# Windowed attention and a gated MLP block: a software pipeline over the batches, long-run loads of q and k, a transposed gating product and sink rows padded to 128

## The chip, the core and the metric

The kernel runs on one core of one Trainium2 chip. The metric is device time in microseconds (us), median of the runs; the kernel before takes 294.75 us (four runs, 294.15 to 295.45). Engines: PE is the tensor engine, PEld its weight loads, DVE the vector engine, ACT the scalar engine, POOL the GpSimd engine, SP the engine that here only issues transfers. In these kernels PE's results go to tiles in PSUM, and its operands lie in tiles in SBUF.

A run is called slow when it is over 1.5% above the fastest run of the same kernel. Times quoted as "measured" are medians of all runs, those marked slow included (the 401 and 452 us below left out); where that matters, the difference by fast runs stands beside it.

## The reference, cut to what matters

Four batches, eight heads, 768 positions, head width 64. Attention sees the last 128 positions and the first four (the sinks). The heads side by side are x (768 x 512 per batch), the input of a gated MLP.

```python
scores = scale * np.matmul(q, k.transpose(0, 1, 3, 2))
keep = is_sink | in_window            # first 4 positions, or 0 <= rel < 128
a = softmax(np.where(keep, scores, -1e9))
x = (a @ v), heads side by side
# gated block
h = gelu_tanh(x @ w_in)               # 512 -> 1024
u, v = h[..., :512], h[..., 512:]
v_n = (v - mean(v)) / np.sqrt(var(v) + 1e-06) * g_ln
v_s = np.einsum('ts,bsd->btd', w_sg, v_n) + b_sg[None, :, None]   # over positions
out = x + (u * v_s) @ w_out
```

(Softmax, gelu and the layer norm are abbreviated here.) q, k and v are drawn with a factor 0.1, so the scores are tiny and the softmax nearly flat.

## The kernel before

Everything is done in phases: attention of all batches, then the transposes of x and w_sg, then the first product of all batches, then the spatial and output products. The parts that the argument touches:

```python
# loads, per head pair: six casting transfers issued by POOL, 256-byte runs
nc.gpsimd.dma_start(
    out=q_sb[:, :, 64 * hl:64 * hl + 64],
    in_=q[b, h0 + hl, :, :].rearrange("(t p) d -> p t d", p=128),
)
# ... k, v likewise
qps = attn_ps.tile([128, S], BF16, name="qps", tag="trp")
for j in range(NT):
    nc.tensor.transpose(qps[:, 128 * j:128 * (j + 1)], q_sb[:, j, :], iden)
nc.vector.tensor_copy(qT, qps)                     # contiguous on both sides
# ... kT likewise, then scores, exp, mask multiply
# the four sink rows: a 4-row score product and 4-row AV products
nc.tensor.matmul(scs[0:n_sink, :], kT[ps, 0:n_sink],
                 qT[ps, 256:768], start=True, stop=True)
# ...
nc.tensor.matmul(av[:, i, :],
                 exs[:, 128 * (i - 2):128 * (i - 1)],
                 v_sb[0:n_sink, hl, 0, :],
                 start=False, stop=last)
```

In the gated block the kernel before applies gelu, `bn_stats` and `bn_aggr` per 128 rows, scales by 1/std in a later pass, forms `gated` with positions on the partitions, and so has to transpose it (96 transposes, 24 copies) before the output product.

The softmax here doesn't subtract the row's maximum and nothing guards it: scores larger than these inputs give would overflow.

Of the kernel before, what the change touches and what calls it, by code (L numbers as in the profile page):

```python
# [8 lines left out]
F32 = mybir.dt.float32  # L10
# [7 lines left out]
def kernel(  # L18
# [23 lines left out]
    assert S % 128 == 0  # L42
# [4 lines left out]
    assert window == 128  # L47
    scale = 1.0 / (Dh ** 0.5)

    consts = ctx.enter_context(tc.tile_pool(name="consts", bufs=1))  # L50
    x_pool = ctx.enter_context(tc.tile_pool(name="x_pool", bufs=1))
# [4 lines left out]
    def build_band_mask(dst, with_sink):  # L56
        nc.gpsimd.memset(dst[:, 0:128], 1.0)
        nc.gpsimd.affine_select(
            out=dst[:, 0:128], in_=dst[:, 0:128], compare_op=ALU.is_ge, fill=0.0,
            base=0, pattern=[[1, 128]], channel_multiplier=-1,  # L60
        )
        nc.gpsimd.memset(dst[:, 128:256], 1.0)
        nc.gpsimd.affine_select(
            out=dst[:, 128:256], in_=dst[:, 128:256], compare_op=ALU.is_ge, fill=0.0,
            base=-1, pattern=[[-1, 128]], channel_multiplier=1,
        )
        if with_sink:
            nc.gpsimd.memset(dst[0:n_sink, :], 1.0)

    m_grp0 = consts.tile([128, 512], BF16)  # L70
    build_band_mask(m_grp0[:, 0:256], True)
    build_band_mask(m_grp0[:, 256:512], False)
    m_grp = consts.tile([128, 512], BF16)
    build_band_mask(m_grp[:, 0:256], False)
    build_band_mask(m_grp[:, 256:512], False)

    x_sb = [x_pool.tile([128, NT, d_model], BF16, name=f"x_{b}") for b in range(B)]

    attn_sb = tc.alloc_tile_pool(name="attn_sb", bufs=2)
    attn_tmp = tc.alloc_tile_pool(name="attn_tmp", bufs=2)  # L80
    attn_ps = tc.alloc_tile_pool(name="attn_ps", bufs=2, space=bass.MemoryType.PSUM)
    attn_ps2 = tc.alloc_tile_pool(name="attn_ps2", bufs=3, space=bass.MemoryType.PSUM)

    for b in range(B):
        for hp in range(HP):
            h0 = 2 * hp
            q_sb = attn_sb.tile([128, NT, 128], BF16, name="q_sb")
            k_sb = attn_sb.tile([128, NT, 128], BF16, name="k_sb")
            v_sb = attn_sb.tile([128, 2, NT, 65], BF16, name="v_sb")
            nc.gpsimd.memset(v_sb[:, :, :, 64:65], 1.0)  # L90

            for hl in range(2):
                nc.gpsimd.dma_start(  # L93
                    out=q_sb[:, :, 64 * hl:64 * hl + 64],
                    in_=q[b, h0 + hl, :, :].rearrange("(t p) d -> p t d", p=128),
                )
                nc.gpsimd.dma_start(  # L97
                    out=k_sb[:, :, 64 * hl:64 * hl + 64],
                    in_=k[b, h0 + hl, :, :].rearrange("(t p) d -> p t d", p=128),
                )  # L100
                nc.gpsimd.dma_start(  # L101
                    out=v_sb[:, hl, :, 0:64],
                    in_=v[b, h0 + hl, :, :].rearrange("(t p) d -> p t d", p=128),
                )

            qT = attn_sb.tile([128, S], BF16, name="qT")
            kT = attn_sb.tile([128, S], BF16, name="kT")
            qps = attn_ps.tile([128, S], BF16, name="qps", tag="trp")
            for j in range(NT):
                nc.tensor.transpose(qps[:, 128 * j:128 * (j + 1)], q_sb[:, j, :], iden)  # L110
            nc.vector.tensor_copy(qT, qps)  # L111
            kps = attn_ps.tile([128, S], BF16, name="kps", tag="trp")
            for j in range(NT):
                nc.tensor.transpose(kps[:, 128 * j:128 * (j + 1)], k_sb[:, j, :], iden)  # L114
            nc.vector.tensor_copy(kT, kps)  # L115

            for hl in range(2):
                ps = slice(64 * hl, 64 * hl + 64)
                h = h0 + hl
                exa = attn_tmp.tile([128, NT, 256], BF16, name="exa", tag="exa")  # L120
                exps = [exa[:, j, :] for j in range(NT)]
                for g in range(NT // 2):
                    j0 = 2 * g
                    sc = attn_ps2.tile([128, 512], F32, name="sc_ps", tag="sc")
                    w = 0
                    for j in (j0, j0 + 1):
                        ncols = 256 if j < NT - 1 else 128
                        nc.tensor.matmul(sc[:, w:w + ncols],  # L128
                                         kT[ps, 128 * j:128 * (j + 1)],
                                         qT[ps, 128 * j:128 * j + ncols],  # L130
                                         start=True, stop=True)
                        w += ncols
                    nc.scalar.activation(out=exa[:, j0:j0 + 2, :].rearrange(  # L133
                        "p a b -> p (a b)")[:, 0:w], in_=sc[:, 0:w],
                        func=AF.Exp, scale=scale)
                    msk = m_grp0 if g == 0 else m_grp
                    nc.vector.tensor_mul(  # L137
                        exa[:, j0:j0 + 2, :].rearrange("p a b -> p (a b)")[:, 0:w],
                        exa[:, j0:j0 + 2, :].rearrange("p a b -> p (a b)")[:, 0:w],
                        msk[:, 0:w])  # L140
                scs = attn_ps2.tile([128, 512], F32, name="scs_ps", tag="sc")
                nc.tensor.matmul(scs[0:n_sink, :], kT[ps, 0:n_sink],  # L142
                                 qT[ps, 256:768], start=True, stop=True)
                exs = attn_tmp.tile([n_sink, 512], BF16, name="exs")
                nc.scalar.activation(out=exs, in_=scs[0:n_sink, :],  # L145
                                     func=AF.Exp, scale=scale)

                av = attn_ps2.tile([128, NT, 65], F32, name="av", tag="av")
                first = True
                for i in range(NT):  # L150
                    nc.tensor.matmul(av[:, i, :], exps[i][:, 0:128],  # L151
                                     v_sb[:, hl, i, :],
                                     start=first, stop=False)
                    first = False
                    if i >= 1:
                        nc.tensor.matmul(av[:, i, :], exps[i - 1][:, 128:256],  # L156
                                         v_sb[:, hl, i - 1, :],
                                         start=False, stop=False)
                    last = (i == NT - 1)
                    if i >= 2:  # L160
                        nc.tensor.matmul(av[:, i, :],  # L161
                                         exs[:, 128 * (i - 2):128 * (i - 1)],
                                         v_sb[0:n_sink, hl, 0, :],
                                         start=False, stop=last)
                    elif last:
                        pass
                rcp = attn_tmp.tile([128, NT, 1], F32, name="rcp")
                nc.scalar.copy(rcp, av[:, :, 64:65])  # L168
                nc.vector.reciprocal(rcp, rcp)  # L169
                nc.vector.tensor_mul(  # L170
                    x_sb[b][:, :, 64 * h:64 * h + 64],
                    av[:, :, 0:64], rcp.to_broadcast([128, NT, 64]),
                )

    attn_tmp.release()
    attn_sb.release()
    attn_ps2.release()
    attn_ps.release()

    w_in_sb = consts.tile([128, KD, d_ff], BF16)  # L180
    nc.gpsimd.dma_start(out=w_in_sb, in_=moe_w_in.rearrange("(c p) f -> p c f", p=128))
    w_out_sb = consts.tile([128, KU, d_model], BF16)
    nc.gpsimd.dma_start(out=w_out_sb, in_=moe_w_out.rearrange("(c p) f -> p c f", p=128))
    g_ln_sb = consts.tile([128, d_half], BF16)
    nc.gpsimd.dma_start(out=g_ln_sb, in_=moe_g_ln.partition_broadcast(128))
    b_sg_sb = consts.tile([128, NT], F32)
    nc.gpsimd.dma_start(out=b_sg_sb, in_=moe_b_sg.rearrange("(t p) -> p t", p=128))
    eps_sb = consts.tile([128, 1], F32)
    nc.vector.memset(eps_sb, 1e-6)

    gconst = ctx.enter_context(tc.tile_pool(name="gconst", bufs=1))
    wsgT = gconst.tile([128, NT, S], BF16)
# [4 lines left out]
    for ti in range(NT):  # L197
# [3 lines left out]
        for si in range(NT):  # L201
            nc.tensor.transpose(wps[:, 128 * si:128 * (si + 1)],
                                wsg_row[:, 128 * si:128 * (si + 1)], iden)
# [119 lines left out]
```

## Time and profile before

| stretch of the trace | what runs | us |
|---|---|---|
| 0 to 13 | start, first loads | 13 |
| 13 to 163 | attention of 16 head pairs, 9.4 us each | 150 |
| 163 to 184 | transposes of w_sg and x | 21 |
| 184 to 228 | first product, gelu, statistics | 44 |
| 228 to 294 | spatial and output products, stores | 66 |

First the page: the busy times, the row with PE's busy tenths, the row with the granted clock, and the chain of waits that ended last (by engine, then by line).

```profile
PE 263.8 (90%) x1545; PEld 129.8 (44%) x1556; DVE 165.1 (56%) x416; ACT 122.6 (42%) x236; POOL 91.1 (31%) x145
PE   0389999999999999999999387999996899999994
PEclk9999999999999999999999999999999799999999
PE 60%; DVE 16%; issue 12%; POOL 6%; DMA 3%; ACT 1%; ACTq 0%; POOLq 0%; DVEq 0%
```

PE is busy nine tenths of the span and has 60% of the chain, so PE bounds this kernel. But a busy PE can still be a slow one. The clock row reads full from the first slice on. The durations contradict it. These two lines are from the view of one tile's instructions (min/median/max in ns, then first and last start); both are 128x128 transposes of x.

```profile
L209 PE MATMUL wps<-iden,x_86 x24: 263/311/311, 174.2 to 177.4; 128*128 128x128 bf16 x24
L209 PE MATMUL wps<-iden,x_87 x24: 216/218/278, 177.5 to 180.2; 128*128 128x128 bf16 x24
```

The same instruction takes 311 ns up to 177.4 us and 218 ns from 177.5 us on. The trace's first clock record, one that reads full, is at 177.7 us; ahead of it there is none, and the row then assumes full speed. The transposes of q and k have a median of 311 ns too, in all of attention from 10.8 to 147.1 us. So the whole attention phase runs at half clock.

The second thing to see is what the four-row sink matmuls cost. The timeline (start in us, duration in us) around one row block of the AV product:

```profile
56.68 0.23 PE L161 MATMUL av<-v_sb,exs 4*128 4x65 bf16 x1
56.84 0.24 PE L151 MATMUL av<-v_sb,exa 128*128 128x65 bf16 x1
56.89 0.24 PE L156 MATMUL av<-v_sb,exa 128*128 128x65 bf16 x1
57.07 0.23 PE L161 MATMUL av<-v_sb,exs 4*128 4x65 bf16 x1
```

The durations overlap, so go by the starts. The two 128-row matmuls start 0.05 us apart; into and out of the four-row one it takes 0.16 to 0.18 us each. A row block takes 0.39 us; three starts 0.05 us apart would be 0.15 us, an estimate.

Last, one line of the groups, for the copy that brings transposed q from PSUM to SBUF (busy us, mean ns of one):

```profile
L111 DVE COPY qT<-qps 128x768 bf16<-128x768 bf16 x16 | 8.8, 550 | 20.2 <-PE qps L110 20.2
```

It takes 0.55 us.

### The profile page before, as it was taken

The numbers are of one execution on the slowest core, as the hardware profiler recorded it, in microseconds if no ns is written. First come the engines' busy times: TensorE is split into PE (matmuls) and PEld (weight loads), VectorE is DVE, ScalarE is ACT, GpSimd is POOL, SyncE is SP. The second block draws the span as 40 slices with busy tenths as digits, with TensorE's granted clock in tenths as the row PEclk, the third lists the DMA queues.
The fourth block names the chain that finished last, engine by engine and source line by source line (L and its number), as shares of the span: only waits on it lengthen the run. The fifth ranks groups of instructions, "written<-read, shape, count | busy, mean of one in ns | idle before, by whom it ended". The sixth has DMA issues, their size and how long they took to land.

```text
span 293.9 us, 4223 instructions
## 1 busy us (share of the span) xinstructions
PE 263.8 (90%) x1545; PEld 129.8 (44%) x1556; DVE 165.1 (56%) x416; ACT 122.6 (42%) x236; POOL 91.1 (31%) x145
## 2 busy tenths in 40 slices
PE   0389999999999999999999387999996899999994
PEld 0234454454445445444544265444442344445551
DVE  0145444364364445544644368499999933358884
ACT  1045545455454554645555000666567255530000
POOL 9993269385559556560301100000000000000000
PEclk9999999999999999999999999999999799999999
DMA  2999699999989899993443300000000000005574
GB/s 14 115 120 161 44 81 111 102 85 73 74 65 98 52 85 67 104 61 21 28 30 54 50 6 0 0 2 1 0 0 2 0 0 0 2 0 214 198 268 180
DMA packets 80836, 18.89 MB, mean 64 GB/s; under 512 B 75824, under 2 KB 77232, under 8 KB 80816
## 3 DMA queue, kind: packets, MB, share of 16 engines
q0 software_dynamic: 77360, 12.33, 57.1%
q1 hardware_dynamic: 3456, 6.29, 5.7%
q8 instruction: 12, 0.20, 0.3%
q14 instruction: 8, 0.07, 0.1%
HBM read 24.64 MB, written 6.29 MB: 105 GB/s over the span
## 4 chain that ended last, share of the span: by engine, by line
PE 60%; DVE 16%; issue 12%; POOL 6%; DMA 3%; ACT 1%; ACTq 0%; POOLq 0%; DVEq 0%
PE sc_ps L128 12%; PE vs_ps L264 11%; PE out_ps L282 7%; PE av L151 6%; DVE stats L242 5%; PE av L161 5%; PE scs_ps L142 4%; PE kps L114 4%; PE qps L110 3%; POOL v_sb L101 2%; PE av L156 2%; PE wps L209 2%; DVE mv L244 2%; POOL k_sb L97 1%; DVE vn_2082 L247 1%
## 5 line engine op out<-in xcount | busy, mean ns | idle before, releaser
L133 ACT ACTIVATE exa<-sc_ps 128x512 bf16<-128x512 f32 (+1 forms) x96 | 52.6, 562 | 44.4 <-PE sc_ps L128 43.7
L128 PE MATMUL sc_ps<-qT,kT 64*128 64x256 bf16 x192 | 54.4, 386 | 0.7 <-DVE kT L115 0.7
L151 PE MATMUL av<-v_sb,exa 128*128 128x65 bf16 x192 | 39.5, 242 | 0.0
L156 PE MATMUL av<-v_sb,exa 128*128 128x65 bf16 x160 | 38.1, 243 | 0.0
L137 DVE TENSOR_TENSOR exa<-exa,m_grp 128x512 bf16<-128x512 bf16 x64 | 24.1, 382 | 17.8 <-ACT exa L133 17.5
L93 POOL DMA_DIRECT2D q_sb<-in_q_dram x32 | 27.4, 858 | 16.1 <-PE qps L110 15.1
L97 POOL DMA_DIRECT2D k_sb<-in_k_dram x32 | 27.3, 859 | 10.4 <-PE qps L110 6.6
L161 PE MATMUL av<-v_sb,exs 4*128 4x65 bf16 x128 | 29.6, 231 | 0.6 <-ACT exs L145 0.6
L151 PEld LDWEIGHTS <-exa 128*128 128x128 bf16 x192 | 19.9, 115 | 18.6 <-issue 7.2
L110 PE MATMUL qps<-iden,q_sb 128*128 128x128 bf16 x96 | 17.4, 305 | 11.5 <-DMA q_sb<-in_q_dram 11.5
L101 POOL DMA_DIRECT2D v_sb<-in_v_dram x32 | 26.6, 840 | 1.3 <-POOL v_sb L90 1.3
L169 DVE RECIPROCAL rcp<-rcp 128x6 f32<-128x6 f32 x32 | 6.1, 192 | 32.4 <-ACT rcp L168 32.4
L264 PEld LDWEIGHTS <-wsgT 128*128 128x128 bf16 x144 | 14.4, 101 | 21.9 <-DVE vn_2082 L254 3.8
L282 PE MATMUL out_ps<-w_out_sb,gatedT 128*128 128x512 bf16 x92 | 22.0, 380 | 1.3 <-DVE gatedT L279 0.9
L137 DVE TENSOR_TENSOR exa<-exa,m_grp_66 128x512 bf16<-128x512 bf16 x32 | 13.6, 424 | 14.7 <-ACT exa L133 13.8
L145 ACT ACTIVATE exs<-scs_ps 4x512 bf16<-4x512 f32 x32 | 18.7, 585 | 5.6 <-PE scs_ps L142 5.2
L128 PEld LDWEIGHTS <-kT 64*128 64x128 bf16 x192 | 15.3, 112 | 12.8 <-issue 3.0
L111 DVE COPY qT<-qps 128x768 bf16<-128x768 bf16 x16 | 8.8, 550 | 20.2 <-PE qps L110 20.2
L168 ACT COPY rcp<-av 128x6 f32<-128x6 f32 x32 | 5.3, 164 | 34.7 <-PE av L161 34.7
L156 PEld LDWEIGHTS <-exa 128*128 128x128 bf16 x160 | 19.7, 124 | 0.0
L114 PE MATMUL kps<-iden,k_sb 128*128 128x128 bf16 x96 | 18.6, 304 | 0.8 <-DMA k_sb<-in_k_dram 0.8
L161 PEld LDWEIGHTS <-exs 4*128 4x128 bf16 x128 | 12.7, 99 | 14.2 <-issue 2.5
(188 smaller groups left out, 399.3 us busy)
## 6 DMA issues: line engine op xcount, KB each, us to landing
out_dram<-out_sb SPq DMA_DIRECT2D x24, 256.0 KB, 2.0
q_sb<-in_q_dram POOLq DMA_DIRECT2D x32, 96.0 KB, 3.4
k_sb<-in_k_dram POOLq DMA_DIRECT2D x32, 96.0 KB, 3.6
v_sb<-in_v_dram POOLq DMA_DIRECT2D x32, 96.0 KB, 3.6
wsg_row<-in_moe_w_sg_dram POOLq DMA_DIRECT2D x6, 192.0 KB, 3.6
w_in_sb<-in_moe_w_in_dram POOLq DMA_DIRECT2D x1, 1024.0 KB, 10.2
w_out_sb<-in_moe_w_out_dram POOLq DMA_DIRECT2D x1, 512.0 KB, 6.2
g_ln_sb<-in_moe_g_ln_dram POOLq DMA_DIRECT2D x1, 128.0 KB, 4.1
```

Source lines behind the costliest of these rows:

```text
L93: nc.gpsimd.dma_start(out=q_sb[:, :, 64 * hl:64 * hl + 64], in_=q[b, h0 + hl, :, :].rearrange("(t p) d -> p t d", p=128),)
L97: nc.gpsimd.dma_start(out=k_sb[:, :, 64 * hl:64 * hl + 64], in_=k[b, h0 + hl, :, :].rearrange("(t p) d -> p t d", p=128),)
L101: nc.gpsimd.dma_start(out=v_sb[:, hl, :, 0:64], in_=v[b, h0 + hl, :, :].rearrange("(t p) d -> p t d", p=128),)
L114: nc.tensor.transpose(kps[:, 128 * j:128 * (j + 1)], k_sb[:, j, :], iden)
L128: nc.tensor.matmul(sc[:, w:w + ncols], kT[ps, 128 * j:128 * (j + 1)], qT[ps, 128 * j:128 * j + ncols], start=True, stop=True)
L133: nc.scalar.activation(out=exa[:, j0:j0 + 2, :].rearrange("p a b -> p (a b)")[:, 0:w], in_=sc[:, 0:w], func=AF.Exp, scale=scale)
L137: nc.vector.tensor_mul(exa[:, j0:j0 + 2, :].rearrange("p a b -> p (a b)")[:, 0:w], exa[:, j0:j0 + 2, :].rearrange("p a b -> p (a b)")[:, 0:w],
L151: nc.tensor.matmul(av[:, i, :], exps[i][:, 0:128], v_sb[:, hl, i, :], start=first, stop=False)
L156: nc.tensor.matmul(av[:, i, :], exps[i - 1][:, 128:256], v_sb[:, hl, i - 1, :], start=False, stop=False)
L161: nc.tensor.matmul(av[:, i, :], exs[:, 128 * (i - 2):128 * (i - 1)], v_sb[0:n_sink, hl, 0, :], start=False, stop=last)
L264: nc.tensor.matmul(vs_ps, wsgT[:, si, 128 * t:128 * (t + 1)], vn_all[b][:, si, :], start=(si == 0), stop=(si == NT - 1))
L282: nc.tensor.matmul(out_ps, gatedT[:, 128 * c:128 * (c + 1)], w_out_sb[:, c, :], start=(c == 0), stop=(c == KU - 1))
```

## The change

The intent, in five parts:

1. **Pipeline over batches.** After batch 0's attention, each batch's spatial and output products are interleaved, unit by unit, with the next batch's attention. The first products (MV for the normed half, MU for the gate half) are interleaved with the transposes of the next batch's q and k (T).
2. **Long-run loads.** q and k are loaded so that partition p holds positions 6p to 6p+5, in runs of 1536 bytes, in f32, by SP; POOL casts them to bf16. The transposed result is then in the wrong order, and the copy out of PSUM puts it right by writing every sixth element.
3. **Transposed gating.** u and the spatial product are computed with features on the partitions, so the gated product needs no transposes. The multiplication by u is done on POOL.
4. **Padded sinks.** The four sink rows of all heads live in zero-padded 128-row tiles, so every AV operand has 128 rows; the row sums come from a head-selecting ones column.
5. 1/std is taken with a power on POOL, per two row blocks, at once.

Below, "first gated stage" is MV and MU of batch 0 with T of batch 1 and the transposes of w_sg; M1, M2, M3 are MV and MU of batches 1 to 3; "mixed" is a spatial and output stage with the next attention.

```diff
 # (cut to the core; the order of pieces is that of the new kernel)
-                nc.gpsimd.dma_start(
-                    out=q_sb[:, :, 64 * hl:64 * hl + 64],
-                    in_=q[b, h0 + hl, :, :].rearrange("(t p) d -> p t d", p=128),
-                )
+        q32 = stage.tile([128, 2, NT * Dh], F32, name="q32")
+        nc.sync.dma_start(out=q32, in_=q[b, hs].rearrange("h (p t) d -> p h (t d)", p=128))
 # ... k32 the same; v32 in short runs
-            nc.vector.tensor_copy(qT, qps)
+            pcast(cb.rearrange("p t h d -> p h t d"),
+                  src.rearrange("p h (t d) -> p h t d", d=Dh))
+            ps = ps_mm.tile([128, NT, 128], BF16, name="trp", tag="mm")
+            for t in range(NT):
+                nc.tensor.transpose(ps[:, t, :], cb[:, t, :, :].rearrange("p h d -> p (h d)"), iden)
+            dst = trs.tile([128, S], BF16, name=name + "T")
+            dv = dst.rearrange("p (i t) -> p t i", t=NT)
+            if name == "q":
+                nc.vector.tensor_copy(dv, ps)
+            else:
+                nc.scalar.copy(dv, ps)
 # ... padded sinks
-                                         exs[:, 128 * (i - 2):128 * (i - 1)],
-                                         v_sb[0:n_sink, hl, 0, :],
+                                 exs[b, p][:, 128 * (i - 2):128 * (i - 1)],
+                                 vsk[:, 2 * p:2 * p + 2, :].rearrange("p h d -> p (h d)"),
 # ... transposed gating
-            nc.scalar.activation(out=gated, in_=vs_ps, func=AF.Identity,
-                                 bias=b_sg_sb[:, t:t + 1])
-            nc.vector.tensor_mul(gated, gated, u_all[b][:, t, :])
-                nc.tensor.transpose(gps[:, 128 * c:128 * (c + 1)],
-                                    gated[:, 128 * c:128 * (c + 1)], iden)
+        nc.vector.scalar_tensor_tensor(out=tmp, in0=ps[:, 0:NH], scalar=g_sb[:, dc:dc + 1],
+                                       in1=b_bc[:, NH * hf:NH * (hf + 1)],
+                                       op0=ALU.mult, op1=ALU.add)
+        nc.gpsimd.tensor_mul(gatedT[b, hf][:, dc, :], tmp, uT[b][:, dc, NH * hf:NH * (hf + 1)])
 # ... the interleave
+        for n, a in enumerate(au):
+            a()
+            while done < ns and done * na < (n + 1) * ns:
+                su[done]()
+                done += 1
```

T, the transposes of w_sg and of x, the sink scores, the spatial and the output products share two PSUM slots (`ps_mm`, two buffers).

## The prediction

> **What bounds the kernel now.** The tensor engine (PE). The chain of waits gives it 60%. By stretches of the trace: attention 13 to 163 us with PE busy over 97%, that is 9.4 us per head pair; weight and x transposes 163 to 184, loosely filled; first product 184 to 228, where the vector engine's statistics chain has the chain of waits (38.7 of 41 us busy); spatial and output products 228 to 294. The load and the statistics are exposed because the phases are serial.
>
> Two things make the attention slow on PE.
> 1. It runs at half clock. The page's clock row says full, but in the timeline four transposes in a row take 0.63 us (311 ns each) up to 177.4 us and 0.38 us (218 ns) from 177.5 us on, so start to start is about 107 ns before and 54 after. Two 64x256 score matmuls start 0.21 us apart, twice what 256 columns need at the later rate (512 columns: 0.216 us).[...]
> 2. The 4-row sink matmuls: in the timeline, AV matmuls of one shape start 0.05 us apart, but going into and out of a sink costs 0.17 us each, so one row block takes 0.39 us. Four per head and 32 heads are 50 us.
>
> **What the change does.** Padded sinks make every AV operand 128 rows: 26 matmuls per pair at about 0.055 us, 1.4 us instead of 3.5. 32 sink score matmuls become 16. The 96 gated transposes and 24 PSUM copies go. Loads go to the SP queue in f32 with 1.5 KB runs for q and k; the casts land on POOL (48 of 768 elements[...]). Statistics and the activation table changes (1.28 us each, 3 become 8) hide under PE work. I expect the dense product matmuls to lift the clock in the first batch's gated block and the mix to keep it lifted, so attention of batches 1 to 3 runs at full clock.
>
> **Sum.** PE per batch at full clock: transposes 4.0, scores 5.0 (48 at 0.11), sinks 0.9, AV 5.7, MV 5.2, MU 5.2, spatial 7.8, out 5.2: 39 us. By stage:
> - start to first score: 9 us (13.6 before);
> - batch 0 attention alone, at half clock, no filler: 4 x 8 = 32;
> - gated first products with next transposes: PE 13, ACT 12, DVE 12, so 17 with waits; three of them 51, the last 12; weight transposes 4;
> - three mixed stages: PE 26, DVE 22, ACT 15[...]: about 29 each, 87;
> - last spatial and output: 16; tail 3.
>
> Total 214; call it **215 us, range 198 to 240**; faster by over 2%: 0.97, within: 0.02, slower: 0.01.
>
> **What would show it.** Transposes about 218 ns and 512-column matmuls 379 ns in mixed stages, about 305 ns in batch 0; AV starts 0.05 us apart through sinks; PE busy over 85% from batch 1's stage on; POOL below 60% of a mixed batch; no wait on loads after the first 10 us; mixed batches near 46 us.
>
> **What would make it wrong.** The clock falling back in mixed stages (attention work costs about twice: +40 us). POOL casts or gating multiplies slower than estimated[...], so transposes wait for casts (+20). Six PSUM-slot pairs too few: in-order PE waiting for exp, mask and copies (+15).[...] Better: row halves of score matmuls overlapping on PE (-8), or batch 0 already at full clock (-10).

The sum of the stages came to 214 us (9 + 32 + 51 + 12 + 4 + 87 + 16 + 3). The limit of 60% for POOL, and that dense products would lift the clock, were estimates; the trace of before doesn't show them. There, full rate came during transposes, at 177.5 us; in e7 it came 5.9 us after the first of 40 dense products. In the changed kernel the records read full from 46.2 to 59.8 us, from 3.7 us into the first gated stage, after two windows of 3.4 us in attention of batch 0.

## The result, and the profile after

The changed kernel takes **246.22 us** (244.83 to 246.97, four runs). Its ratio to the kernel before is **0.835** (95% interval 0.831 to 0.839). Ratios in this document are the mean time of one kernel's fast runs over that of the other's of the same rounds, so not quite the ratio of the medians that are quoted. The change is clearly faster, but 31 us slower than the 215 predicted, and above the range.

The page of the kernel after, the same kinds of lines as shown of before:

```profile
PE 182.6 (74%) x1460; PEld 99.1 (40%) x1460; DVE 178.5 (73%) x302; ACT 135.2 (55%) x123; POOL 96.5 (39%) x134
PE   0457557892959979798478869898559698978892
PEclk9999875798575999999855999999889999999999
DVE 37%; PE 27%; ACT 13%; POOL 8%; issue 6%; DMA 5%; SPq 2%; POOLq 0%; DVEq 0%; ACTq 0%
DVE qT L168 10%; DVE pt L206 9%; ACT kT L170 7%; PE hv L254 6%; PE ops L307 6%; POOL gatedT L301 5%; DVE z L271 5%; DMA v_104<-in_v_dram 4%; DVE gtmp L298 4%; ACT pt L204 4%; PE sc L199 3%; DVE st L265 3%; PE vs L294 3%; DVE ot L310 3%; PE scs L184 2%
```

PE's busy time fell from 263.8 to 182.6 us: the tensor work got cheaper, as hoped. But the chain is no longer PE's. DVE has 37% of it, and its first entry is the copy of qT, with the copy of kT in third place. The groups show why:

```profile
L168 DVE COPY qT<-trp 128x768 bf16<-128x768 bf16 x16 | 43.5, 2718 | 12.4 <-PE trp L164 12.2
L170 ACT COPY kT<-trp 128x768 bf16<-128x768 bf16 x16 | 43.6, 2725 | 13.8 <-PE trp L164 13.8
L301 POOL TENSOR_TENSOR gatedT<-gtmp,uT 128x384 bf16<-128x384 bf16 x32 | 33.2, 1042 | 64.8 <-DVE gtmp L298 62.7
```

The copy that took 550 ns takes 2718 ns, on both engines, with the same number of elements and the same types. Only the order in which it writes has changed. The 32 copies cost 87 us of DVE and ACT together.

The stages, from the view of busy time by stretch (stretch and length in us, then busy time with count of PE, PEld, DVE, ACT, POOL, then granted clock, DMA share and GB/s). The lines are: attention of batch 0; first gated stage; mixed; M1; mixed; M2; mixed; M3; last spatial and output.

```profile
11.20:42.50 31.30, 20.38 (x191) 11.48 (x192) 21.91 (x34) 21.83 (x21) 13.20 (x15) 0.84 1.04 237
42.50:78.20 35.70, 26.97 (x183) 15.93 (x181) 28.45 (x44) 22.87 (x18) 14.91 (x20) 0.74 0.81 206
78.20:104.20 26.00, 22.22 (x231) 12.68 (x230) 20.14 (x38) 10.95 (x13) 13.04 (x13) 0.96 0.28 86
104.20:132.20 28.00, 21.05 (x126) 10.69 (x123) 21.50 (x34) 20.73 (x16) 11.79 (x17) 0.80 0.56 147
132.20:159.00 26.80, 23.08 (x236) 12.57 (x236) 21.39 (x39) 12.63 (x15) 9.68 (x9) 0.95 0.11 40
159.00:184.60 25.60, 18.59 (x125) 9.95 (x121) 20.33 (x34) 19.77 (x15) 5.90 (x10) 0.93 0.06 21
184.60:210.00 25.40, 21.70 (x235) 12.18 (x235) 21.18 (x39) 13.32 (x16) 8.74 (x8) 1.00 0.11 42
210.00:224.80 14.80, 13.10 (x75) 6.49 (x73) 7.77 (x20) 8.28 (x9) 2.39 (x6) 1.00 0.10 38
224.80:245.30 20.50, 13.86 (x69) 6.03 (x66) 9.90 (x16) 0.81 (x1) 7.52 (x9) 0.97 0.21 77
```

Set against the terms of the prediction's sum, which came to 214:

| stage | predicted | measured | difference |
|---|---|---|---|
| start to first score | 9 | 11.2 | +2.2 |
| batch 0 attention | 32 | 31.3 | -0.7 |
| first gated stage, with w_sg transposes | 17 + 4 | 35.7 | +14.7 |
| M1 | 17 | 28.0 | +11.0 |
| M2 | 17 | 25.6 | +8.6 |
| M3 | 12 | 14.8 | +2.8 |
| three mixed stages | 87 | 78.2 | -8.8 |
| last spatial and output, tail | 19 | 20.5 | +1.5 |
| sum | 214 | 245.3 | +31.3 |

The whole miss, and more, lies in the gated stages. In M1 the prediction had PE at 13 us, ACT 12 and DVE 12; the line above has 21.0, 20.7 and 21.5.

How copies on DVE and ACT stop PE is seen in the timeline of the first gated stage. The last column of the third line is the idle time of PE ahead of it and what ended it.

```profile
58.38 2.72 DVE L168 COPY qT<-trp 128x768 bf16<-128x768 bf16 x1
58.98 2.72 ACT L170 COPY kT<-trp 128x768 bf16<-128x768 bf16 x1
61.15 0.80 PE L164 MATMUL trp<-iden,kb 128*128 128x128 bf16 x6 [4.89 <-DVE qT L168]
```

PE wants to transpose the next k. Both PSUM slots hold transposes that wait for their copy or are being copied out, in steps of six elements. In the trace the gate product that follows in the program starts only at 61.75, after this transpose, so PE stands still for 4.89 us, until the copy that began at 58.38 is done. The copy is 2.72 us of these; in the first 2.1 us DVE still worked on the statistics and on z, so this stop isn't the copies' alone (e1 below has one like it). M1 shows a cleaner one:

```profile
117.06 2.74 DVE L168 COPY qT<-trp 128x768 bf16<-128x768 bf16 x1
117.66 2.72 ACT L170 COPY kT<-trp 128x768 bf16<-128x768 bf16 x1
119.85 0.49 PE L164 MATMUL trp<-iden,qb 128*128 128x128 bf16 x6 [3.79 <-DVE qT L168]
```

M2 has the same stop, 3.77 us up to 174.57. The records of the granted clock then show what follows such a pause: full rate from 46.2, half from 59.8 to 66.7 us and again from 70.1 to 80.3, from 121.3 to 134.9 (from M1 on) and from 175.9 to 179.3 us (M2). Between the first record at 25.7 us and the end of the span the kernel spends 48.9 us at half clock.

The padded sinks behave as intended. Row blocks through a sink, in a mixed stage (L229 is the sink):

```profile
143.78 0.23 PE L229 MATMUL av<-v_sink_143,exs 128*128 128x130 bf16 x1
143.84 0.19 PE L219 MATMUL av<-v_sb_145,pt 128*128 128x65 bf16 x1
143.87 0.19 PE L225 MATMUL av<-v_sb_145,pt 128*128 128x65 bf16 x1
143.90 0.19 PE L219 MATMUL av<-v_sb_145,pt 128*128 128x65 bf16 x1
143.93 0.19 PE L225 MATMUL av<-v_sb_145,pt 128*128 128x65 bf16 x1
143.96 0.22 PE L229 MATMUL av<-v_sink_143,exs 128*128 128x130 bf16 x1
144.11 0.39 PE L199 MATMUL sc<-qT,kT 64*128 64x256 bf16 x4
```

Starts are 0.03 us apart, into the sink as well, and 0.06 out of it (the sink now serves both heads), where it was 0.16 to 0.18. In the last line four score matmuls of 256 columns take 0.39 us together: they start in pairs, 0.003 us apart within a pair and 0.12 us from pair to pair, so the two row halves overlap. The step from the 128-row sink to these 64-row score matmuls still takes 0.15 us.

### The profile page after: what moved, and what is told of

Same layout as the page of the kernel before. It is cut to its first block, busy times and chain, and to the rows that moved or that the text cites. A ratio compares the mean times of both kernels' runs of the same rounds, so it can differ in the third digit from the quotient of the medians.

```text
span 245.3 us, 3835 instructions
## 1 busy us (share of the span) xinstructions
PE 182.6 (74%) x1460; PEld 99.1 (40%) x1460; DVE 178.5 (73%) x302; ACT 135.2 (55%) x123; POOL 96.5 (39%) x134
## 2 busy tenths in 40 slices
DMA packets 39778, 28.59 MB, mean 117 GB/s; under 512 B 26576, under 2 KB 36048, under 8 KB 39760
## 4 chain that ended last, share of the span: by engine, by line
DVE 37%; PE 27%; ACT 13%; POOL 8%; issue 6%; DMA 5%; SPq 2%; POOLq 0%; DVEq 0%; ACTq 0%
DVE qT L168 10%; DVE pt L206 9%; ACT kT L170 7%; PE hv L254 6%; PE ops L307 6%; POOL gatedT L301 5%; DVE z L271 5%; DMA v_104<-in_v_dram 4%; DVE gtmp L298 4%; ACT pt L204 4%; PE sc L199 3%; DVE st L265 3%; PE vs L294 3%; DVE ot L310 3%; PE scs L184 2%
## 5 line engine op out<-in xcount | busy, mean ns | idle before, releaser
L204 ACT ACTIVATE pt<-sc 128x1024 bf16<-128x1024 f32 (+1 forms) x48 | 43.7, 954 | 27.6 <-PE sc L199 27.4
L301 POOL TENSOR_TENSOR gatedT<-gtmp,uT 128x384 bf16<-128x384 bf16 x32 | 33.2, 1042 | 64.8 <-DVE gtmp L298 62.7
L168 DVE COPY qT<-trp 128x768 bf16<-128x768 bf16 x16 | 43.5, 2718 | 12.4 <-PE trp L164 12.2
L170 ACT COPY kT<-trp 128x768 bf16<-128x768 bf16 x16 | 43.6, 2725 | 13.8 <-PE trp L164 13.8
L294 PE MATMUL vs<-wsgT,z 128*128 128x384 bf16 x192 | 38.6, 339 | 2.3 <-DVE z L271 1.1
L307 PE MATMUL ops<-w_out_sb,gatedT 128*128 128x512 bf16 x96 | 26.9, 381 | 11.8 <-POOL gatedT L301 10.3
L281 PE MATMUL hu<-xT,w_in_sb 128*128 128x384 bf16 x128 | 28.4, 373 | 0.5 <-ACT uT L284 0.2
L298 DVE SCALAR_TENSOR_TENSOR gtmp<-vs,g_sb,b_bc 128x384 bf16<-128x384 f32 x32 | 19.5, 610 | 12.0 <-PE vs L294 12.0
L254 PE MATMUL hv<-w_in_sb,xT 128*128 128x512 bf16 x96 | 24.6, 392 | 3.0 <-ACT vt L260 2.1
L206 DVE TENSOR_TENSOR pt<-pt,mask_128 128x1024 bf16<-128x1024 bf16 (+1 forms) x32 | 25.8, 817 | 0.9 <-ACT pt L204 0.4
L199 PE MATMUL sc<-qT,kT 64*128 64x256 bf16 x192 | 22.0, 305 | 4.4 <-ACT kT L170 4.2
L294 PEld LDWEIGHTS <-z 128*128 128x128 bf16 x192 | 17.7, 100 | 18.0 <-issue 6.9
L310 DVE TENSOR_TENSOR ot<-ops,x_sb 128x512 f32<-128x512 f32 x24 | 16.4, 689 | 11.2 <-PE ops L307 11.2
L164 PE MATMUL trp<-iden,qb 128*128 128x128 bf16 x96 | 10.2, 255 | 15.5 <-DVE qT L168 7.6
## 6 DMA issues: line engine op xcount, KB each, us to landing
w_in_sb<-in_moe_w_in_dram POOLq DMA_DIRECT2D x1, 1024.0 KB, 11.2
```

The source lines that it names most:

```text
L168: nc.vector.tensor_copy(dv, ps)
L170: nc.scalar.copy(dv, ps)
L199: nc.tensor.matmul(sc[:, hl, 256 * jl:256 * jl + n], kT[b, p][rows, 128 * j:128 * (j + 1)], qT[b, p][rows, 128 * j:128 * j + n], start=Tru ...
L204: nc.scalar.activation(out=pt[:, :, 0:w], in_=sc[:, :, 0:w], func=AF.Exp, scale=scale)
L206: nc.vector.tensor_mul(pt[:, :, 0:w], pt[:, :, 0:w], m.unsqueeze(1).to_broadcast([128, 2, w]))
L254: nc.tensor.matmul(hp[:, jl, :], xT[b][:, c, 128 * j:128 * (j + 1)], w_in_sb[:, c, d_half:2 * d_half], start=(c == 0), stop=(c == KD - 1))
```

## The experiments

The main theory: the un-permuting copies take 2.7 us instead of under 1, hold the two PSUM slots and so stop PE in the gated stages, and the clock falls because PE stops. The rivals: the clock falls back by itself, whatever the copies do; or the loads, or POOL's casts and multiplications, hold the stages up. The texts use letters for these; each says what its letters expect.

### 1. e1_perm_on_read: the same permutation, made on the reading side

```diff
-            dv = dst.rearrange("p (i t) -> p t i", t=NT)
+            dv = dst.rearrange("p (i t) -> p i t", t=NT)
+            pv = ps.rearrange("p t i -> p i t")
-                nc.vector.tensor_copy(dv, ps)
+                nc.vector.tensor_copy(dv, pv)
-                nc.scalar.copy(dv, ps)
+                nc.scalar.copy(dv, pv)
```

Each element goes to the same place as before; only the loop order of the copy differs. It now reads PSUM in steps and writes SBUF without a gap.

> Same values, but the two un-permuting copies per head pair write SBUF contiguously and take the 6-way permutation on the PSUM read side. Theory A (the writes with a step of 12 bytes cost 3.5 ns per element, so each copy takes 2.72 us instead of about 0.95): copies fall to 0.8 to 1.1 us, the three gated-block stages with transposes fall from 25 us to about 17, total 215 to 225 us. Rival B (permuting costs the same whichever side has the step): copies stay near 2.7 us and the time stays at 246. Rival C (the stages are long because the clock falls back, whatever the copies cost): copies fall, but the total falls by less than 10 us.

Measured: 223.92 us (220.3 to 225.72; the upper two of four are slow), ratio 0.752 (0.747 to 0.758), correct. That is 22 us less by the medians and 24 by the ratios of fast runs, from one index order. The groups of its page:

```profile
L169 DVE COPY qT<-trp 128x768 bf16<-128x768 bf16 x16 | 15.2, 950 | 15.4 <-PE trp L164 15.3
L171 ACT COPY kT<-trp 128x768 bf16<-128x768 bf16 x16 | 12.9, 806 | 11.1 <-PE trp L164 11.1
```

The copies fell from 2718 and 2725 ns to 950 and 806. Two stretches of the same view as above, M1 and the mixed stage after it:

```profile
91.60:114.10 22.50, 17.07 (x125) 9.27 (x122) 16.62 (x34) 13.31 (x16) 12.22 (x17) 1.00 0.70 182
114.10:139.20 25.10, 21.81 (x238) 12.26 (x236) 20.89 (x39) 12.81 (x15) 10.63 (x9) 1.00 0.12 43
```

M1 went from 28.0 to 22.5 us with its clock at 1.00 instead of 0.80, and M2 from 25.6 to 19.5: the copies' part of the expectation came true, the stages' "about 17" did not. The half clock after the first record, within the span, went from 48.9 us to 10.7 us, although nothing was done to the clock. PE's longest stop in M1 fell from 3.79 to 1.59 us. The other traces agree: between 85 us and the last 3 us of the span, the three with slow copies (the changed kernel, e16, and e4 in its longer run) spend 10 to 17 us at half clock, the seven interleaved kernels with cheap copies and long runs (e1, e2, e5, e10, e12, e13, e18) none. (e3 with short runs has 3.4 us there, e15 without the interleave 10.2.) So in M1 and M2 the fallen clock came with the slow copies and the stops of PE, and was not a separate cause. In the first 85 us the windows of half clock differ more between kernels, and one trace of each can't tell chance from cause. By stage, the 26.7 us between the two profiled spans (245.3 and 218.6) are: start 1.3, batch 0 7.1, first gated stage 3.3, M1 5.5, M2 6.1, all the rest 3.4. In batch 0 the clock also lifted earlier, at 13.3 instead of 25.7 us, but the record shows that this isn't what made it shorter: in e16, with slow copies, it lifted at 14.4 us and batch 0 took 32.6 us; in e2, with cheap ones, it lifted at 13.9 and batch 0 took 24.5.

The first gated stage gained only 3.3 us. It still has a long stop, of which the copy (0.96 us here) is a small part: DVE waited 3.70 us for 1/std from POOL, which came behind casts that waited for loads.

```profile
50.83 1.50 DVE L272 TENSOR_SCALAR z<-vt,mv,rs 128x512 bf16<-128x512 f32 x2 [3.70 <-POOL rs L270]
53.76 0.49 PE L164 MATMUL trp<-iden,kb 128*128 128x128 bf16 x6 [4.75 <-DVE qT L169]
```

### 2. e2_no_perm_wrong: no permutation at all (wrong)

```diff
-            dv = dst.rearrange("p (i t) -> p t i", t=NT)
+            dv = dst.rearrange("p (t i) -> p t i", t=NT)
```

> Wrong result on purpose: the copies are contiguous on both sides, so queries and keys stay in a permuted order; loads, masks and all sizes as in the changed kernel. This is the bound for what the un-permuting copy costs. Theory A: each copy 0.55 to 0.85 us, total 210 to 220 us, half-clock time in the gated-block stages much reduced. Rival C: total above 235.

Measured: 219.38 us (217.68 to 222.04, the last slow), ratio 0.748 (0.743 to 0.753). The copies take 552 ns on DVE and 805 on ACT. So reading in steps costs DVE 0.40 us a copy and ACT nothing, and together that is worth at most a few us (the two intervals overlap). e1 has nearly all there is to gain from the copies.

This kernel scrambles the positions of q and k and was still found correct. The scores are so small that the softmax hardly depends on them. A "correct" says little about the order of positions. For e1 that doesn't matter, since its mapping is that of the changed kernel element by element.

### 3. e3_short_runs: undo the long runs

```diff
-        nc.sync.dma_start(out=q32, in_=q[b, hs].rearrange("h (p t) d -> p h (t d)", p=128))
+        nc.sync.dma_start(out=q32.rearrange("p h (t d) -> p (h t) d", d=Dh),
+                          in_=q[b, hs].rearrange("h (t p) d -> p (h t) d", p=128))
 # ... k32 the same; the copies contiguous on both sides, as in e2
```

> Right result: q and k are loaded in 256-byte runs again (as in the kernel before), copies contiguous on both sides. About 41000 more DMA packets of 38 ns over 16 engines, about 95 us more of mean DMA busy time of 16 engines. Theory A: the packets hide in the later batches and cost at most a few us at the start, total 212 to 225 us, so the long runs bought little and cost over 20 us. Rival D (the long runs are needed, loads become the wait): total over 235, with transposes waiting for loads.

Measured: 236.22 us (234.95 to 238.4), ratio 0.803 (0.798 to 0.808). Correct, but slower than I expected: the expectation was missed. The trace counts 80738 packets instead of 39778, and the first gated product starts at 48.2 us instead of 34.2 in e2. Loads are the limit at the start, and short runs make it worse. Two things follow. The long runs are worth 17 us (236.22 against e2's 219.38). And as the change made them, with the strided write, they lost more than that: the changed kernel without them is 10 us faster than with them.

### 4. e4_stride_probe: what does a strided copy cost by itself?

Sixteen copies of 768 elements per partition, SBUF to SBUF, were put ahead of the changed kernel, with output steps of 1, 2, 3, 6 and 16 elements in bf16 and 1, 2 and 6 in f32, on each engine.

```diff
+    nc.vector.tensor_copy(d16v[:, 0:768 * 6].rearrange("p (n s) -> p n s", s=6)[:, :, 0], psrc)
+    nc.scalar.copy(d16s[:, 0:768 * 6].rearrange("p (n s) -> p n s", s=6)[:, :, 0], psrc)
 # ... and the other steps and types
```

> Measures the disputed cost by itself: at the start, 768-element copies from contiguous SBUF to SBUF on the vector and on the scalar engine, bf16 with destination step 1, 2, 3, 6 and 16 elements and f32 with step 1, 2 and 6. Theory A: bf16 with step 2 or more takes about 2.7 us on both engines whatever the step; f32 with a step stays near its contiguous time, if the cost is of writes below a word, or rises too if it is of any scattered write. Rival B: SBUF-sourced steps cost no more than contiguous ones (0.3 to 0.9 us). The total time rises by the probes and says nothing.

From the view of one tile's instructions, steps 1 and 6 on DVE, then on ACT:

```profile
L58 DVE COPY d16v<-psrc x1: 296/296/296, 2.0 to 2.0; 128x768 bf16<-128x768 bf16 x1
L61 DVE COPY d16v<-psrc x1: 1445/1445/1445, 5.0 to 5.0; 128x768 bf16<-128x768 bf16 x1
L68 ACT COPY d16s<-psrc x1: 832/832/832, 2.1 to 2.1; 128x768 bf16<-128x768 bf16 x1
L71 ACT COPY d16s<-psrc x1: 2750/2750/2750, 7.9 to 7.9; 128x768 bf16<-128x768 bf16 x1
```

All steps, in us:

| output step, elements | 1 | 2 | 3 | 6 | 16 |
|---|---|---|---|---|---|
| DVE, bf16 | 0.296 | 0.595 | 0.801 | 1.445 | 1.842 |
| ACT, bf16 | 0.832 | 1.049 | 1.462 | 2.750 | 3.395 |
| DVE, f32 | 0.548 | 0.543 | | 0.855 | |
| ACT, f32 | 0.829 | 0.884 | | 1.597 | |

On ACT the step of six, 2750 ns, explains the kernel's 2725 ns fully: no rival work is needed. The cost grows with the step, so the expectation, about 2.7 us whatever the step, was missed. f32 at a step of two costs DVE nothing (0.543 against 0.548 us), so DVE's doubling in bf16 from step 1 to 2 may have another cause than the later growth; that wasn't separated. In bf16 a step of 2 already costs ACT a quarter more (1.049 against 0.832 us) and a step of 6 over three times as much. The distance in bytes alone doesn't set the cost: f32 at a step of six, twice as far, took less than bf16, 0.855 against 1.445 us on DVE and 1.597 against 2.750 on ACT. On DVE, one question is left open: from SBUF the step of six takes 1.445 us, and in the kernel, from PSUM, 2.718. The probe didn't cover a PSUM source.

### 5. e5_load_order: give the next batch's q, k and v precedence over the weights

On top of e1: the sink rows in one transfer instead of eight, and the loads of w_sg and w_out held back: they are issued after batch 1's, and one-element copies on POOL make each wait until a k of batch 1 has landed.

```diff
-        for h in range(H):
-            nc.sync.dma_start(out=t[n_sink * h:n_sink * (h + 1), :], in_=v[b, h, 0:n_sink, :])
+        nc.sync.dma_start(out=t, in_=v[b, :, 0:n_sink, :])
 # ...
     def load_rest():
+        nc.gpsimd.tensor_copy(wsg_rows[:, 0, 0:1], staged[1, 1][1][:, 0, 0:1])
+        nc.gpsimd.tensor_copy(w_out_sb[:, 0, 0:1], staged[1, 2][1][:, 0, 0:1])
 # ...
-    load_rest()
     load_sinks(1)
     for p in range(HP):
         load(1, p)
+    load_rest()
```

> e1_perm_on_read plus another order of the loads: the eight sink rows of a batch in one DMA instead of eight, and the spatial weights, output weights and broadcast bias only after the loads of batch 1. Theory L (in e1 the first gated block takes 27 us instead of 18 because batch 1's q and k come late: the SP queue stands 10 us behind the sink loads and the bias load, and 3.4 MB of weights share the DMA engines): the first gated block, first product to first score, falls from 27 to 18 to 21 us, total 212 to 218 us. Rival: the DMA engines are simply full until 60 us (31 MB in all) and order doesn't matter: total 222 to 226.

Measured: 231.06, 230.52, 233.04 (all slow) and 225.77 us; no gain: missed. The trace (231.06 us) shows a stall. The one small sink transfer stood behind 2.4 MB of other loads and landed 11.45 us after it was issued. POOL waited 9.5 us for it and did its next casts only after that. The clock lifted for the first time at 48.2 us and the first gated product started at 47.0.

### 6. e6_before_padded and e6b_before_padded: the padded sinks alone

Into the kernel before, only the sinks were padded to 128 rows with zeros.

```diff
-                nc.tensor.matmul(scs[0:n_sink, :], kT[ps, 0:n_sink],
+                nc.tensor.matmul(scs, ksp[hp % 2][ps, :],
                                  qT[ps, 256:768], start=True, stop=True)
 # ...
-                                         v_sb[0:n_sink, hl, 0, :],
+                                         vsp[hp % 2][:, hl, :],
```

> One part of the change alone, on the kernel before: sink keys and values padded with zeros to 128 rows, so that no matmul of attention has a 4-row stationary or moving operand. Theory A (going into and out of a 4-row matmul costs 0.17 us each on PE): a row block of three AV matmuls falls from 0.39 us to 0.16 to 0.20, total 265 to 275 us at the half clock. If the 4-row matmuls were also what kept the clock low: transposes of attention fall from 0.31 to 0.22 us and the total is 240 to 260. Rival: the PE was waiting on something else there and the time stays above 290.

Measured: 267.96, 268.1 and 268.54 us, ratio 0.911 (0.905 to 0.916), so 26.5 us from this alone, as expected. One of its four runs, the profiled one, took 452.07 us; it is left out. The profile was taken again as e6b:

> The kernel of e6_before_padded again, only for a profile of an undisturbed run (its profiled run fell into a state with 450 us). About 268 us; transposes of attention about 0.31 us (half clock) and AV starts about 0.055 us apart without the 0.17 us steps around sinks. If the transposes take 0.22 us, padding also lifted the clock and part of its 26 us is that.

e6b took 270.68 us (one look). In its trace the AV matmuls start 0.05 to 0.06 us apart through the sinks (L168 is the sink):

```profile
99.06 0.25 PE L163 MATMUL av<-v_sb,exa 128*128 128x65 bf16 x1
99.12 0.24 PE L168 MATMUL av<-vsp,exs 128*128 128x65 bf16 x1
99.17 0.24 PE L158 MATMUL av<-v_sb,exa 128*128 128x65 bf16 x1
```

The transposes of attention still take 314 ns in the median, and the first clock record comes at 150.6 us, after attention. So padding removes the slow steps around the sinks and does not lift the clock.

### 7. e7_before_warm: would a warm start keep the clock up in the old attention?

```diff
+    warm = consts.tile([128, 512], BF16, name="warm")
+    nc.vector.memset(warm, 0.5)
+    wp = attn_ps2.tile([128, 512], F32, name="wp", tag="sc")
+    for _ in range(40):
+        nc.tensor.matmul(wp, warm[:, 0:128], warm, start=True, stop=True)
```

> Kernel before with 40 dense 128x128 by 128x512 matmuls of constants ahead of attention, in the time in which PE waits for the first load (and about 6 us beyond, if they run at half clock). Theory A (the attention work of the kernel before does not hold the clock): the clock lifts during the burst and falls back within about 15 us, the transposes of attention are 0.31 us again, total 295 to 302 us. Rival (it only never had the dense work that lifts the clock): transposes stay at 0.22 us through attention, total 240 to 265.

Measured: 295.29 us (one look), no gain. The clock lifts at 7.4 us, 5.9 us after the first of the dense matmuls, and falls back at 17.7 us, soon after attention begins. The stretch from there to its next lift:

```profile
17.00:174.70 157.70, 151.20 (x940) 75.72 (x937) 77.43 (x202) 73.98 (x157) 74.80 (x106) 0.50 0.95 72
```

PE counts as busy for 151.2 of 157.7 us, yet the granted clock is 0.50 throughout. The old attention does not hold the clock even when it is given it. The traces show two rates (transposes of 311 and 218 ns in the kernel before); the lift took 5.9 us here; and three falls in the changed kernel came during or just after stops of PE of 3.77 to 4.89 us. But in e7 it fell although PE's longest stop after the dense matmuls was 0.78 us, and stayed down at 96% busy. In the kernel before, on the other hand, it lifted while PE ran nothing but transposes, from 164.4 us on (311 ns up to 177.4 us, 218 ns from 177.5). So the profile's busy share alone doesn't tell the clock here. What kept it down in attention, no run here shows.

### 8. e9_serial: e1 without the interleave

```diff
             a()
-            while done < ns and done * na < (n + 1) * ns:
-                su[done]()
-                done += 1
         for s in su[done:]:
             s()
```

> e1_perm_on_read without the interleave: the next batch's whole attention first, then this batch's spatial and output products; all else the same. It measures what the interleave itself is worth. PE need of a mixed stage is 26 us and it takes 28 to 30; apart, attention is bound by ACT (15 us) and by waits, about 19 us, and the spatial and output products take about 17: 6 to 7 us more per batch, three times: total 240 to 246. If the interleave is worth nothing: 220 to 228.

Measured: 227.21 and 226.25 us, 232.43 (slow), and 401.19 in the profiled run, which is left out; ratio 0.770 (0.764 to 0.776). Against e1's ratio of 0.752 that is about 5 us ((0.7697 - 0.7522) x 294.7; the two ran on different chips), where I had expected 16 to 22: missed. The headline part of the change, interleaving attention with the products, was worth little at this point. The next three runs show what held it.

### 9. e10_sinks_early, e12_gate_dve_last, e13_gate_dve_all: POOL in the mixed stages

e10 is e5 with the sink rows loaded right behind the first q, k and v. e12 and e13 are e10 with the multiplication by u moved from POOL to DVE, in the last batch only or in all.

```diff
 # e10
     load(0, 0)
-    load(0, 1)
     load_sinks(0)
+    load(0, 1)
 # e13
-        nc.gpsimd.tensor_mul(gatedT[b, hf][:, dc, :], tmp, uT[b][:, dc, NH * hf:NH * (hf + 1)])
+        nc.vector.tensor_mul(gatedT[b, hf][:, dc, :], tmp, uT[b][:, dc, NH * hf:NH * (hf + 1)])
```

> e5_load_order with the one sink load of batch 0 issued right after the first q, k, v. In e1 and e5 POOL stood still until 17 us for the sink rows, which were behind 2.4 MB of loads, and every later cast waited. Theory P (this and the load order are what is left of my miss): POOL's wait for the sink rows falls from 6 us to under 2, first product at 30 to 36 us instead of 47 (e5), first spatial product at 58 to 62 instead of 66 to 76, total 211 to 218 us. Rival (DMA engines full until 60 us): first spatial product stays at 66 or later, total 220 to 226.

e10: 223.22 us (222.9 to 226.22), ratio 0.760 (0.754 to 0.765): it repairs e5, but is no better than e1: missed. The first spatial product starts at 68.5 us (66.5 in e1). Over the first 60 us the transfers move 268 GB/s and keep their engines filled (the view's DMA share reads 1.10), and POOL waits for loads of v, which are still in 256-byte runs, once for 10.72 us. Reordering did not help here, which fits a limit by the sum of the loads.

> e10 plus the eight gating multiplies of the last batch on the vector engine (about 0.35 us each from its 512-element mask multiply of 0.42) instead of POOL (1.04 us). The last stage, which has no attention beside it, waits for POOL: 2 to 4 us less than e10. Rival (POOL's multiplies hide behind PE): within 1 us of e10.

e12: 221.01 us (220.46 to 221.47), ratio 0.750 (0.746 to 0.753), 2 us better than e10.

> e10 plus all 32 gating multiplies on the vector engine. POOL loses 33 us, the vector engine gains 11 us; its mask multiplies, 0.79 us now, fall to about 0.65 if POOL's two-input work on SBUF slowed them. Theory: output matmuls wait less for the gated tile, 4 to 8 us less than e10. Rival (the vector engine is the bound of the mixed stages): same as e12 or slower.

e13: 213.43 us (211.42 to 214.65), ratio 0.722 (0.716 to 0.727): 10 us better than e10 (11 by the ratios), more than the 4 to 8 expected. Its profiled run, 214.65 us, is slow, just above the limit. A mixed stage of it, to be held against the second line of e1 above:

```profile
115.50:135.70 20.20, 19.74 (x211) 11.10 (x211) 18.60 (x43) 12.65 (x15) 0.00 (x0) 1.00 0.11 40
```

DVE has more instructions (43 instead of 39) and less busy time (18.6 instead of 20.9 us), and the stage takes 20.2 us instead of 25.1. Part of the difference is work that slides into the next stage; the whole period of a batch, first product to first product, goes from 47.6 to 43.6 us. How can DVE get faster with more work? Its mask multiplications show it (min/median/max in ns). After:

```profile
L206 DVE TENSOR_TENSOR pt<-pt,mask_128 x32: 509/676/2198, 17.1 to 204.7; 128x1024 bf16<-128x1024 bf16 x16, 128x768 bf16<-128x768 bf16 x16
```

e13:

```profile
L206 DVE TENSOR_TENSOR pt<-pt,mask x48: 548/682/1311, 13.9 to 174.6; 128x1024 bf16<-128x1024 bf16 x32, 128x768 bf16<-128x768 bf16 x16
```

The medians are alike, the tail isn't: 2198 against 1311 ns. Sorting the 1024-wide ones of the kernel after by whether an instruction of POOL overlaps them gives a mean of 0.70 us for the 12 that are alone and 1.06 for the 20 that are not; in e13 the 27 alone have 0.68. So a mask multiplication lasts longer where POOL works at the same time; by what mechanism, no run here shows. Over all 48 of them the mean falls from 808 ns in e10 to 683 in e13. e13 also removes a hop from DVE to POOL and on to PE. How much each of the two is worth was not separated.

### 10. e15_serial_gate_dve: e13 without the interleave

The edit is that of e9, on e13.

> e13_gate_dve_all without the interleave of attention and gated block (as e9 was to e1). In e13 a mixed stage takes 20 to 21 us. If the interleave hides ACT's 15 us behind PE's 20, as I had it, the serial version pays 5 us or more per mixed stage: 228 to 235. If the finer overlap inside each part does the same, as e9 hints: 213 to 219.

Measured: 222.7 us (221.56 to 225.27), ratio 0.756 (0.752 to 0.760), 9 us slower than e13 (10 by the ratios), between the two expectations. So the interleave is worth 9 to 10 us with POOL's multiplications out of the way and about 5 with them, which suggests that the two parts depended on each other. The two pairs of kernels also differ in the order of loads and ran on different chips.

### 11. e16_after_gate_dve: is that a second, separate cause?

The edit of e13 alone, on the changed kernel as it was.

> The changed kernel with only the gating multiplies moved from POOL to the vector engine; the slow copies stay. If POOL's multiplies alone explain the miss: 215 to 225. If they are a second cause, which adds to the copies: 236 to 242. If they matter only once the copies are cheap: 244 to 247.

Measured: 237.19 and 234.82 us, 240.77 and 240.73 (slow), ratio 0.803 (0.796 to 0.809), median 238.96. That is 7 us below 246.22 by the medians and 9.5 by the ratios of fast runs, with the copies' code unchanged. The multiplications on POOL are a second cause, which adds to the first.

### 12. e18_first_casts: a better version

On e13, the very first q is cast by DVE and the first k by ACT, since POOL is still building masks and constants then.

```diff
+            fast = {"q": nc.vector.tensor_copy, "k": nc.scalar.copy}[name]
+            (fast if (b, p) == (0, 0) else pcast)(
+                cb.rearrange("p t h d -> p h t d"),
+                src.rearrange("p h (t d) -> p h t d", d=Dh))
```

> e13_gate_dve_all with the very first q cast on the vector engine and the first k cast on ACT, which are idle then, so that they need not wait for POOL to build the masks. First score at 7 us instead of 9.3, total 1 to 3 us less than e13. Rival (the loads of the first 60 us bound the start): within 1 us of e13.

Measured: **208.83 us** (207.87 to 209.89), ratio **0.710** (0.706 to 0.715), correct. The first score comes at 8.7 us. It gained 4.6 us on e13 by the medians, 3.4 by the ratios, where 1 to 3 were expected, and the first score was expected at 7 us; the runs of the two come from different chips and their clock windows differ, so the excess isn't explained. This beats both kernels and lies inside the range that was predicted for the change.

## Why the prediction was wrong

The direction was right, the size was not: 246.2 us is above the 198 to 240 given.

**The step that failed** is the term "gated first products with next transposes: PE 13, ACT 12, DVE 12, so 17 with waits; three of them 51". Judging by its DVE 12 and ACT 12, it had the un-permuting copies at no more than about their old price; they were never given a term of their own. They measured 2.72 us each, 4 on DVE and 4 on ACT in each of these stages, five times the 0.55 us of before. Both engines then had about 21 us to do in M1, PE stood still behind two occupied PSUM slots (3.79 us in M1, 3.77 in M2), and the clock fell to half 1.4 and 1.3 us after these stops. M1 and M2 took 28.0 and 25.6 us instead of 17. e1 undoes nothing but the order of writing, and the kernel takes 223.9 us, inside the range. The prediction had looked at the diff's `rearrange` on that copy as if it were free.

The copies are not all of it. In e1's profiled run the gated stages take 32.4, 22.5, 19.5 and 14.7 us, still 22 us above the prediction's 67, while batch 0 (24.2 instead of 32) and the mixed stages (74.9 instead of 87) are 20 us below theirs. So it is partly luck that e1's sum comes out near 214: errors in both directions cancel. In M1 the other work of DVE was set too low as well: 16.6 us in e1, or 15 with the copies at 0.55 (an estimate: 4 x 0.40 less), against 12. What the rest of the excess in M1 and M2 waits for was not tested.

**A second cause** is POOL's part in the mixed stages. Measured, POOL was busy for 13.0, 9.7 and 8.7 us of the three stages. A cast took 0.83 us in the median. The multiplications by u take 1.04 us each, 33 us in all, overlap with slower masks on DVE (1.06 against 0.70 us), and stand between DVE and PE in every output product. Moving them gave 7 us on the changed kernel (e16) and 10 on e10 (e13) by the medians, 9.5 and 11 by the ratios. The text did list "gating multiplies slower than estimated" among the things that could go wrong.

**"No wait on loads after the first 10 us" was wrong.** In the changed kernel POOL waits 7.48 us for a sink row until 17.8 us, and even in e1 the first gated stage takes 32.4 us at 292 GB/s, where 21 were predicted. e3 and e10 point to the load as the limit there until about 60 us; in part it acts through POOL, whose 1/std comes behind casts that wait for loads. Against the 22.5 us of e1's M1, with 4 us for the w_sg transposes, the excess is 6 us, an estimate.

**The clock was half right.** It did lift and it stayed up in the mixed stages (0.96, 0.95, 1.00). It fell in the gated stages (0.74, 0.80, 0.93), which the text had not named. PE was busy for 85 to 86% of the mixed stages, as told, but for 73 to 76% of the first three gated ones.

**Right:**
- Attention of before at half clock although the page reads full (e7 and the durations).
- The four-row sinks: AV starts are 0.03 to 0.06 us apart after, and e6 gives 26.5 us for that part alone.
- The last stage at 19 us (20.5). Batch 0 at 32 us (31.3) is luck: the 31.3 hold six slow copies that the prediction didn't have, and without them it takes 24.2 (e1).
- POOL below 60% of a mixed batch: 21.5 of 54.8 us.
- The mixed stages, a little better than told: 78.2 us instead of 87. The "better" case, row halves of the scores overlapping on PE, was seen: four matmuls of 256 columns in 0.39 us.
- "Mixed batches near 46 us": 54.8 and 51.0 us from first product to first product in the changed kernel, but 47.6 and 44.2 in e1, once the copies are cheap.

**What stays open:** why DVE's strided copy takes 2.72 us from PSUM and 1.45 from SBUF; what keeps the clock at half in attention of before; the windows of half clock in the first 85 us, which differ from kernel to kernel; why times of one kernel spread by 2%; and the executions of 401 us (e9) and 452 us (e6), whose pages have no clock row and whose 512-column output matmuls take 0.85 and 0.83 us in the mean, against 0.38 in the kernels before and after.

## What to carry to other kernels

When a load's layout is changed to get long runs, the permutation comes back in some later instruction: find that instruction, give it a term of its own and price it by its write order. If it must be made in a copy out of PSUM, read in steps and write without gaps; here that took 0.81 to 0.95 us instead of 2.72 and was worth 22 to 24 us. And before taking a busy tensor engine for a fast one, compare the durations of one instruction in two places of the trace, and look for what stops it, because here a stop of 3.8 us cost twice: the wait itself, and the half clock after it.
